# Top-32 attention and a cosine-gated feed-forward on one core: another way of searching the scores, and split, gates and second product at other places of the slot

## The chip, the cores and the metric

The kernel runs on one core of one Trainium2 chip. The metric is the device time of one execution in microseconds (us): the median of three runs.

## The reference

Scores are formed for 8 batches of 8 heads with 576 queries and 576 keys of 64 numbers. In each row all but the 32 largest scores are masked out; the row goes through a softmax and is multiplied with v. The result, 4608 tokens of 512 numbers, goes through two products with a gate between them.

```python
def _attn_ref(q, k, v):
    scores = scale * np.matmul(q, k.transpose(0, 1, 3, 2))
    kth = np.partition(scores, -top_k, axis=-1)[..., -top_k:-top_k + 1]
    scores = np.where(scores >= kth, scores, -1000000000.0)
    scores = scores - np.max(scores, axis=-1, keepdims=True)
    attn = np.exp(scores)
    attn = attn / (np.sum(attn, axis=-1, keepdims=True) + 1e-09)
    return np.matmul(attn, v)

def _moe_ref(x, w_in, w_out):          # 4608 x 512, 512 x 2048, 2048 x 512
    h = x @ w_in
    g = h * np.cos(h)
    return g @ w_out
```

## The kernel before, in words

**Units, slots and blocks.** A unit is 128 queries of a pair of heads: 144 units. A block is the 128 tokens of four units (36 blocks); the feed-forward works by blocks. The program is a list of 144 slots, one for each unit, written out by hand in `slot` (the schedule is manual: each engine gets its instructions in the order of the code, and an instruction that waits holds up all that stand behind it on its engine). In slot i the unit u = i is searched, the unit w = i - 1 is masked and exponentiated, the unit x = i - 2 is split, and parts of the feed-forward of earlier blocks are laid between, by the remainder m of i by four. Slots of remainder 0 to 3 are called s0 to s3 below.

**Scores.** TensorE forms the scores of two units in each even slot (`scores`, L242); a score buffer of a unit is free again when VectorE has folded it. ScalarE copies them into SBUF (`take_scores`, L253 and L257) at the end of the slot before the search.

**The search.** A row of 576 scores is folded at its middle: the larger of each pair by VectorE straight from the score buffer (`fold_high`, L267), the smaller by GpSimd as sum minus larger, in whole numbers (`fold_sum` L283, `fold_low` L292), or by VectorE in the three slots of `BUSY`, in which weights are still being decoded (`fold_now`, L275). The instruction MAX8 gives the eight largest of a row, MATCH_REPLACE8 strikes them out (`search`, L361 and L366). The 288 larger ones are searched four times for eight, 32 in all, and the 288 smaller ones twice, 16 in all; two reductions over pairs of the two sorted lists (`merge_first` L349, `merge_second` L354) give the 32nd of all, the threshold. GpSimd's smaller half is wanted late, when the larger half has been searched through.

**Mask, exponentials, split.** ScalarE masks (L380) and exponentiates (L389, with the sum of the row), loading its table anew when a sine stood between. VectorE forms sum and reciprocal (L397, L402) in the last search of the slot. `send` then runs at the start of the next slot but one after the search: GpSimd splits the weights into 16-bit halves (L412) and copies the reciprocal beside them (L418), SP writes the halves out (L446), issues loads of later q, k and v, and reads the halves back transposed into a ring of five places (L452). The first units go through TensorE instead (`turn`).

**P@V and the feed-forward.** In s2 TensorE multiplies the four units of a block with v (`values`, L480), and VectorE scales them into xT (L496, L504). The first product of a block has four banks of 64 matmuls (`first_bank`, L543); ScalarE takes each bank twice, as h / 2 pi and rounded to a whole number (`take_first`, L557 and L559); GpSimd forms the argument (`argument`, L572 and L575), ScalarE the sine of two banks at a time (`sine`, L583), GpSimd the gate, which overwrites the bank (`gate`, L592). The second product has four runs of 16 matmuls, one for each gated bank (`second_run`, L606), and is taken out and stored by ScalarE (`take_second`, L616 and L618). Banks and second product share two PSUM buffers. The order of the feed-forward of one block over the slots before the change:

| slot | first product | second product | GpSimd |
|---|---|---|---|
| s2 | bank 0 | | |
| s3 | bank 1 | | |
| s0 | bank 2 | | arguments 0, 1 |
| s1 | bank 3 | run 0 | gates 0, 1, argument 2 |
| s2 | | run 1, behind P@V of the next block | argument 3, gates 2, 3 |
| s3 | | run 2 | |
| s0 | | run 3, then taken out | |

Of the kernel before, what the change touches and what calls it, by code (L numbers as in the profile page):

```python
# [10 lines left out]
F32 = mybir.dt.float32  # L11
I32 = mybir.dt.int32
# [3 lines left out]
ALU = mybir.AluOpType  # L16
# [14 lines left out]
def kernel(  # L31
# [218 lines left out]
    def take_scores(u):  # L250
# [7 lines left out]
        if at:  # L258
            nc.scalar.copy(out=s[:, :, 0:at], in_=u["sc"][:, :, 0:at])  # L259

    def fold_high(u):

        s, sc = u["s"], u["sc"]
        if u["n"] not in BUSY:
            del u["sc"]
        u["rest"] = work.tile([P, 2, S], F32, tag="rest", name="rest", bufs=1)
        nc.vector.tensor_tensor(  # L267
            out=u["rest"][:, :, HS:S], in0=sc[:, :, 0:HS], in1=s[:, :, HS:S], op=ALU.max
        )

    def fold_now(u):

        s, sc = u["s"], u.pop("sc")
        u["low"] = work.tile([P, 2, HS], F32, tag="low", name="low", bufs=1)
        nc.vector.tensor_tensor(  # L275
            out=u["low"], in0=sc[:, :, 0:HS], in1=s[:, :, HS:S], op=ALU.min
        )

    def fold_sum(u):

        s = u["s"].bitcast(I32)
        u["low"] = work.tile([P, 2, HS], F32, tag="low", name="low", bufs=1)
        nc.gpsimd.tensor_tensor(  # L283
            out=u["low"].bitcast(I32), in0=s[:, :, 0:HS], in1=s[:, :, HS:S], op=ALU.add
        )

    def fold_low(u):

        if u["n"] in BUSY:
            return  # L290
        low = u["low"].bitcast(I32)
        nc.gpsimd.tensor_tensor(  # L292
            out=low, in0=low, in1=u["rest"][:, :, HS:S].bitcast(I32), op=ALU.subtract
        )

    dens = []
    for i in range(2):
# [3 lines left out]

    tops = []
    for i in range(2):
        t = consts.tile([P, 2, TOPK + 1, 2], F32, tag=f"top{i}", name=f"top{i}")
        nc.vector.memset(t[:, :, 0, 1], -NEG)
        tops.append(t)

    def topk_first(u, w, ahead=()):  # L310

        u["top"] = tops[u["n"] % len(tops)]
        if w:
            merge_first(w)
        for step in ahead:
            step()
        if u["n"] not in BUSY:
            fold_sum(u)
        fold_high(u)
        if w:  # L320
            merge_second(w)
        if u["n"] in BUSY:
            fold_now(u)
        topk_round(u, 0, [lambda: distances(w), lambda: None] if w else ())

    def topk_round(u, rnd, between=(), ahead=None):
        top, rest, lasts = u["top"], u["rest"], TOPK // 8 - 1
        end = TOPK - 1 - 8 * rnd
        at = top[:, :, end : end - 8 if rnd < lasts else None : -1, 0]
        search(  # L330
            at, rest[:, :, HS:S] if rnd == 0 else rest[:, :, 0:HS], rest[:, :, 0:HS], rnd < lasts,
            between if rnd < lasts else (),
        )
        if rnd < lasts:
            return
        del u["rest"]
        low = u.pop("low")
        for k in range(TOPK // 16):
            more = k < TOPK // 16 - 1
            if ahead and not more:  # L340
                ahead()
            search(top[:, :, 1 + 8 * k : 9 + 8 * k, 1], low, low, more, () if more else between)

    def merge_first(u):
        n = TOPK // 2 + 1
        u["lesser"] = u["top"].rearrange("p j r i -> p j (r i)")[:, :, 2 * n : 3 * n]
        nc.vector.tensor_reduce(  # L349
            out=u["lesser"], in_=u["top"][:, :, 0:n], axis=mybir.AxisListType.X, op=ALU.min  # L350
        )

    def merge_second(u):
        nc.vector.tensor_reduce(  # L354
            out=u["top"][:, :, TOPK - 1, 1], in_=u.pop("lesser"), axis=mybir.AxisListType.X,
            op=ALU.max, negate=True,
        )

# [7 lines left out]
                nc.vector.match_replace(rest[:, j], to[:, j], src[:, j], NEG)  # L366

    def distances(u):
        top = u.pop("top").rearrange("p j r i -> p j (r i)")
        u["less"] = top[:, :, 2 * TOPK - 1 : 2 * TOPK]  # L370
        u["nd"] = small.tile([P, 2], F32, tag="nd", name="nd")
        nc.vector.tensor_reduce(
            out=u["nd"], in_=top[:, :, 2 * TOPK - 2 : 2 * TOPK], axis=mybir.AxisListType.X, op=ALU.add
        )

    def mask(u):
# [27 lines left out]
    def both(u):  # L404
        return [lambda: sums(u), lambda: reciprocal(u)] if u else ()

    def split_scores(u):
# [4 lines left out]
        nc.gpsimd.tensor_copy(out=halves[:, :, 0 : 2 * S], in_=s.rearrange("p (k h) -> p h k", h=2))  # L412

    def split_sums(u):

        halves = u["halves"]
        rden = u.pop("rden").bitcast(U16).rearrange("p (j h) -> p h j", h=2)
        nc.gpsimd.tensor_copy(  # L418
            out=halves[:, :, 2 * S :].rearrange("p h (j d) -> p h j d", j=2),
            in_=rden.unsqueeze(3).to_broadcast([P, 2, 2, D]),  # L420
        )
# [216 lines left out]
    at_slot, at_once = {}, {}  # L638

    def load_at(i, *what):  # L640
        while i in at_slot or (what[0] is load_v and i % NP == 0):
            i += 1
        at_slot[i] = what

# [17 lines left out]
    for i, u in enumerate(units):  # L662
        u["n"] = i

    def send(x, between=()):

        split_scores(x)
        split_sums(x)
        for step in between:
            step()  # L670
        write_halves(x)
        for load, b, hp in at_send.pop(x["n"] + 2, ()):
            load(b, hp)
        transposes(x)

    def slot(i, u, w, x, z):
        m, b = i % NP, (i - NP - 2) // NP
        n = (3, 4, 3, 4, 4, 3, 2, 2, 0, 2, 2, 0)[i] if i < 3 * NP else 0
# [12 lines left out]
        topk_round(u, 1)  # L691
        topk_round(u, 2)
        if i > 1:
            decode_second(NP)
            decode_third()

        for o in scored.get(i, []):
# [54 lines left out]
        decode_first(NP)  # L752

    def drain():

        b = NB - 2
        ff["end"] = True
        w, x, last_two = units[NU - 1], units[NU - 2], units[NU - 2 :]
        send(x)
        argument(b, 0)  # L760
        second_run(b - 1, 3)
        merge_first(w)
        merge_second(w)
        distances(w)
        mask(w)
        exponentials(w)
        sums(w)
# [1 line left out]
        send(w)  # L769
        take_first(b, 1)  # L770
        argument(b, 1)
        first_bank(b, 2)
        sine(b, 0)
        gate(b, 0)
        gate(b, 1)
        take_second(b - 1)
        take_first(b, 2)
        first_bank(b, 3)
        argument(b, 2)
        second_run(b, 0)  # L780
        take_first(b, 3)
# [2 lines left out]
        sine(b, 1)  # L784
        gate(b, 2)
        gate(b, 3)
        values(units[NU - 4 : NU - 2])
        take_values(units[NU - 4 : NU - 2])
        second_run(b, 2)
        values(last_two)  # L790
        take_values(last_two)
        second_run(b, 3)
        b += 1
        first_bank(b, 0)
        take_second(b - 1)
        take_first(b, 0)
        argument(b, 0)
        for k in range(1, BANKS):
            first_bank(b, k)
            take_first(b, k)  # L800
            argument(b, k)
            if k % 2 == 1:
                sine(b, k // 2)
                gate(b, k - 1)
                gate(b, k)
# [55 lines left out]
```

## Time and profile before

| | |
|---|---|
| median of three runs | 1406.32 us (1405.22 to 1406.49) |
| the profiled execution | 1406.25 us |
| its span on the core | 1404.1 us |
| granted TensorE clock, mean | 0.985 |
| ScalarE busy | 1140.7 us (81%) |
| GpSimd busy | 1197.8 us (85%) |

The busy time of TensorE is modelled from pipelined matmuls; whether it stands still is read from the starts of its groups. A row of the timeline gives start and length in us, engine, line, operation, tiles, shape and count, and in brackets the idle time before it with what ended it. A row of the stretches gives the stretch, its length, and the busy time of TensorE, its weight loads, VectorE, ScalarE and GpSimd with their numbers of instructions, then granted clock, DMA share and GB/s. A grouped row gives line, engine, operation, tiles and shape with its count, then busy time and mean ns of one, then idle time before. PE is TensorE, DVE VectorE, ACT ScalarE, POOL GpSimd, SP SyncE.

### The profile page before, as it was taken

The page shows a single profiled execution, that of the slowest core. Times are in us where ns is not written, and L with a number is a line of the kernel's source. Part 1 is how long each engine was busy: PE and PEld are TensorE (multiplying, and loading weights), DVE is VectorE, ACT ScalarE, POOL GpSimd, SP SyncE. Part 2 cuts the span into 40 slices and gives each one's busy share as a digit, 9 for nine tenths or more (in the row PEclk, how much of TensorE's full clock was granted, in tenths as well). Part 3 has the DMA queues.
Part 4 walks back from the last instruction along what each step waited for, and adds up shares of the span by engine and source line. Part 5 has one row for each costly group of instructions (what it writes and reads, how often), then busy time and mean ns, then how long its engine had stood idle before and what let it go on. Part 6 is the DMA issues. An engine that isn't in the chain of part 4 may idle for free.

```text
span 1404.1 us, 43874 instructions
## 1 busy us (share of the span) xinstructions
PE 1347.3 (96%) x17024; PEld 906.3 (65%) x17024; DVE 1337.5 (95%) x5012; ACT 1140.7 (81%) x2043; POOL 1197.8 (85%) x1008
## 2 busy tenths in 40 slices
PE   5569999999999999999999999999999999999998
PEld 3355666666666666666666666666666666776665
DVE  7998999999999999999999999999999999999941
ACT  6978888888888888888888888888888888888842
POOL 4787999999999999999999999999999999999920
PEclk9789999999999999999999999999999999999999
DMA  9567775768566586767756568666768566555640
GB/s 285 191 195 188 191 191 152 200 177 200 165 167 168 158 195 172 182 166 176 193 165 176 151 171 198 165 176 163 207 169 175 145 165 172 156 155 144 159 121 16
DMA packets 427488, 240.87 MB, mean 172 GB/s; under 512 B 375952, under 2 KB 392592, under 8 KB 427280
## 3 DMA queue, kind: packets, MB, share of 16 engines
q1 hardware_dynamic: 420720, 224.22, 61.2%
q10 hardware_dynamic: 6560, 13.85, 3.0%
q8 instruction: 133, 2.18, 0.7%
q14 instruction: 75, 0.61, 0.1%
HBM read 45.09 MB, written 101.19 MB: 104 GB/s over the span
## 4 chain that ended last, share of the span: by engine, by line
DVE 68%; ACT 18%; PE 8%; POOL 3%; issue 1%; DMA 1%; ACTq 0%; POOLq 0%; DVEq 0%
DVE top L361 32%; DVE rest L366 18%; DVE rest L267 7%; DVE low L366 6%; ACT s L389 4%; ACT s L380 4%; PE o L606 3%; ACT L583 3%; PE mm L543 3%; ACT x L583 2%; ACT s L253 2%; PE rim L480 2%; ACT s L257 2%; DVE xT L496 1%; DMA ring<-rows 1%
## 5 line engine op out<-in xcount | busy, mean ns | idle before, releaser
L543 PEld LDWEIGHTS mm<-xT,w_in 128*64 128x64 f32 x9216 | 509.5, 137 | 68.2 <-issue 30.3
L543 PE MATMUL mm<-xT,w_in 128*64 128x128 f32 x9216 | 523.7, 273 | 2.7 <-ACT x L559 1.7
L606 PE MATMUL o<-w_out,g 128*64 128x512 f32 x2304 | 521.8, 595 | 3.1 <-POOL g L592 3.1
L361 DVE MAX8 top<-rest 128x8 f32<-128x288 f32 x1152 | 478.9, 451 | 0.0
L366 DVE MATCH_REPLACE8 rest<-top,rest 128x288 f32<-128x288 f32 x864 | 376.6, 443 | 0.0
L380 ACT ACTIVATE s<-s,top 128x576 f32<-128x576 f32 x288 | 207.7, 769 | 189.0 <-DVE top L354 130.3
L606 PEld LDWEIGHTS o<-w_out,g 128*64 128x64 f32 x2304 | 160.6, 137 | 257.6 <-issue 253.2
L412 POOL COPY halves<-s 128x2304 uint16<-128x2304 uint16 x140 | 294.6, 2104 | 35.7 <-ACT s L389 22.3
L361 DVE MAX8 top<-low 128x8 f32<-128x288 f32 x576 | 241.8, 449 | 1.5 <-POOL low L292 1.5
L389 ACT ACTIVATE s<-s,nd 128x576 f32<-128x576 f32 x288 | 220.8, 769 | 2.2
L292 POOL TENSOR_TENSOR low<-low,rest 128x576 int32<-128x576 int32 x141 | 199.8, 1417 | 11.0
L283 POOL TENSOR_TENSOR low<-s 128x576 int32<-128x576 int32 x141 | 200.0, 1418 | 6.5 <-ACT s L259 6.5
L592 POOL TENSOR_TENSOR g<-g,x 128x512 f32<-128x512 f32 x136 | 172.5, 1279 | 16.4 <-ACT x L583 16.4
L575 POOL TENSOR_TENSOR x<-g,x 128x512 f32<-128x512 f32 x136 | 174.0, 1279 | 11.4
L242 PE MATMUL sc<-k,q 64*64 64x448 f32 (+1 forms) x1120 | 147.9, 568 | 14.4 <-DMA k<-in_k_dram 7.4
L480 PE MATMUL rim<-ring,v 128*64 128x128 f32 (+1 forms) x2560 | 138.8, 267 | 0.2 <-issue 0.2
L480 PEld LDWEIGHTS rim<-ring,v 128*64 128x64 f32 x2560 | 129.5, 139 | 6.8 <-issue 6.3
L253 ACT COPY s<-sc 128x896 f32<-128x896 f32 (+1 forms) x144 | 128.0, 889 | 3.4 <-PE sc L242 3.4
L366 DVE MATCH_REPLACE8 low<-top,low 128x288 f32<-128x288 f32 x288 | 125.4, 443 | 0.0
L267 DVE TENSOR_TENSOR rest<-sc,s 128x576 f32<-128x576 f32 x144 | 107.7, 748 | 6.8 <-ACT s L259 6.8
L257 ACT COPY s<-rim 64x256 f32<-64x256 f32 (+1 forms) x280 | 102.8, 367 | 6.9 <-PE rim L480 5.2
L242 PEld LDWEIGHTS rim<-k,q 64*64 64x64 f32 (+1 forms) x1120 | 49.0, 139 | 75.6 <-issue 60.1
(55 smaller groups left out, 1210.1 us busy)
## 6 DMA issues: line engine op xcount, KB each, us to landing
rows<-halves SPq DMA_DIRECT2D x140, 640.0 KB, 3.5
out_dram<-ob ACTq DMA_DIRECT2D x36, 256.0 KB, 3.9
q<-in_q_dram SPq DMA_DIRECT2D x31, 288.0 KB, 5.0
st<-in_moe_w_in_dram SPq DMA_DIRECT2D x16, 512.0 KB, 6.9
v<-in_v_dram SPq DMA_DIRECT2D x32, 256.0 KB, 4.4
k<-in_k_dram SPq DMA_DIRECT2D x31, 144.0 KB, 4.5
k<-in_k_dram SPq DMA_DIRECT2D x32, 128.0 KB, 4.4
st<-in_moe_w_out_dram SPq DMA_DIRECT2D x8, 512.0 KB, 5.6
```

What stands on the lines that cost most here:

```text
L242: nc.tensor.matmul(to[r0 : r0 + rows, rim_bank(r0, j) if k0 else place(u["hp"], j), 0 : k1 - k0], st["q"][d, q0 : q0 + rows], st["k"][d, k ...
L267: nc.vector.tensor_tensor(out=u["rest"][:, :, HS:S], in0=sc[:, :, 0:HS], in1=s[:, :, HS:S], op=ALU.max)
L283: nc.gpsimd.tensor_tensor(out=u["low"].bitcast(I32), in0=s[:, :, 0:HS], in1=s[:, :, HS:S], op=ALU.add)
L292: nc.gpsimd.tensor_tensor(out=low, in0=low, in1=u["rest"][:, :, HS:S].bitcast(I32), op=ALU.subtract)
L361: nc.vector.max(to[:, j], src[:, j])
L366: nc.vector.match_replace(rest[:, j], to[:, j], src[:, j], NEG)
L380: nc.scalar.activation(out=s[:, j], in_=s[:, j], func=AF.Prelu, bias=less[:, j], scale=1.0, alpha=FAR)
L389: nc.scalar.activation(out=s[:, j], in_=s[:, j], func=AF.Exp, bias=nd[:, j : j + 1], scale=SCALE, accum_out=den[:, j, 0:1],)
L412: nc.gpsimd.tensor_copy(out=halves[:, :, 0 : 2 * S], in_=s.rearrange("p (k h) -> p h k", h=2))
L480: nc.tensor.matmul(to[d, r], lhsT, rhs, start=(bank, j) not in begun, stop=c == NT - 1 and u in us[-2:] and r0 + rows == P,)
L543: nc.tensor.matmul(mm[r0 : r0 + D, a * P : (a + 1) * P], w_in[f // FC][:, c, (f % FC) * P + r0 : (f % FC) * P + r0 + D], blk["xT"][:, c], ...
L606: nc.tensor.matmul(blk["o"][r0 : r0 + D], g[:, at : at + D], w_out[f], start=f == 0, stop=f == NF - 1)
```

## The change

The larger half is searched twice for eight, with the rest of it written beside the smaller half; what is left of both, 576 numbers in one tile `rest`, is then searched twice for eight more. The 32nd found is the threshold, and one reduction, which changes its sign, takes the place of the two merges. The smaller half is wanted from the third search on. The smaller half is folded by VectorE in every s1 too (`by_vector`).

`send` is called for w instead of x, at the end of the slot of its exponentials. In the feed-forward, runs 0 and 1 of the second product both stand in s1, run 2 in s2 behind P@V, run 3 in s3, and the second product is taken out at the start of ScalarE's work in s0. In s2 the call of run 2 stands ahead of the sine and the gate of its bank, so the run multiplies that bank (a quarter of the 2048 columns) without the cosine, and the gate comes after. In s3, bank 0 is taken out ahead of the mask; in s0, `sine` and the taking of bank 2 stand behind the copy of the scores. The drain after the last slot follows the same order.

```diff
+    def by_vector(u):
+        return u["n"] in BUSY or u["n"] % NP == 1 and u["n"] > NP + 2
...
-    def topk_first(u, w, ahead=()):
+    def topk_first(u, w):
         u["top"] = tops[u["n"] % len(tops)]
+        u["rest"] = work.tile([P, 2, S], F32, tag="rest", name="rest", bufs=1)
         if w:
-            merge_first(w)
-        for step in ahead:
-            step()
-        if u["n"] not in BUSY:
+            threshold(w)
+        if not by_vector(u):
             fold_sum(u)
         fold_high(u)
-        if w:
-            merge_second(w)
-        if u["n"] in BUSY:
+        if by_vector(u):
             fold_now(u)
-        topk_round(u, 0, [lambda: distances(w), lambda: None] if w else ())
+        search(
+            u["top"][:, :, 1:9], u["high"], u["rest"][:, :, 0:HS], True,
+            [lambda: distances(w), lambda: None] if w else (),
+        )

     def topk_round(u, rnd, between=(), ahead=None):
...
+        if ahead:
+            ahead()
+        some = u["rest"][:, :, 0 : HS if rnd == 1 else S]
+        search(u["top"][:, :, 1 + 8 * rnd : 9 + 8 * rnd], some, some, rnd < TOPK // 8 - 1, between)
...
+    def threshold(u):
+        u["less"] = u["top"][:, :, 0:1]
         nc.vector.tensor_reduce(
-            out=u["lesser"], in_=u["top"][:, :, 0:n], axis=mybir.AxisListType.X, op=ALU.min
-        )
...
+            out=u["top"][:, :, 0], in_=u["top"][:, :, TOPK : TOPK + 1], axis=mybir.AxisListType.X,
             op=ALU.max, negate=True,
         )
...
     def slot(i, u, w, x, z):
...
-        if x:
-            (turn if i < NP + 2 else send)(x)
-        if m == 1:
-            gate(b, 0)
-        elif m == 0:
-            argument(b, 0)
-        topk_first(u, w, [lambda: argument(b - 1, 3)] if m == 2 else ())
+        if x and i < NP + 2:
+            turn(x)
+        topk_first(u, w)
         fold_low(u)
...
         if z:
             values(z)
-        if m == 1:
+        if m == 0:
+            take_second(b - 1)
+            first_bank(b, 2)
+        elif m == 1:
+            gate(b, 0)
             gate(b, 1)
-        elif m == 0:
+            argument(b, 2)
+            first_bank(b, 3)
+            second_run(b, 0)
+            second_run(b, 1)
+        elif m == 2:
+            second_run(b - 1, 2)
+        else:
             second_run(b - 1, 3)
-        elif m == 2:
-            second_run(b - 1, 1)
-        elif m == 3:
-            second_run(b - 1, 2)
+            take_first(b, 0)
+            first_bank(b, 1)

         if w:
             mask(w)
+        if m == 2:
+            sine(b - 1, 1)
+            gate(b - 1, 2)
+            gate(b - 1, 3)
+        if w:
+            exponentials(w)
         if m == 0:
             take_first(b, 1)
             argument(b, 1)
-            first_bank(b, 2)
         elif m == 1:
-            take_first(b, 2)
-            argument(b, 2)
-            first_bank(b, 3)
-            second_run(b, 0)
-        if w:
-            exponentials(w)
-        if m == 3:
-            take_first(b, 0)
-        elif m == 2:
-            sine(b - 1, 1)
-            gate(b - 1, 2)
-            gate(b - 1, 3)
+            take_first(b, 3)
         if i + 1 < NU:
             take_scores(units[i + 1])
+        if m == 0:
+            sine(b, 0)
+            take_first(b, 2)
...
         topk_round(u, 3, both(w), ahead)
...
-        if m == 2:
+        if w and i > NP:
+            send(w)
+        if m == 1:
+            argument(b, 3)
+        elif m == 2:
             first_bank(b, 0)
         elif m == 3:
-            first_bank(b, 1)
-        elif m == 0:
-            sine(b, 0)
-            take_second(b - 1)
-        elif m == 1:
-            take_first(b, 3)
+            argument(b, 0)
         decode_first(NP)
```

More of the change, by code (lines that the diff above doesn't have):

```diff
@@ L259, in take_scores @@
             nc.scalar.copy(out=s[:, :, 0:at], in_=u["sc"][:, :, 0:at])
+    def by_vector(u):
+        return u["n"] in BUSY or u["n"] % NP == 1 and u["n"] > NP + 2
     def fold_high(u):
         s, sc = u["s"], u["sc"]
-        if u["n"] not in BUSY:
+        if not by_vector(u):
             del u["sc"]
-        u["rest"] = work.tile([P, 2, S], F32, tag="rest", name="rest", bufs=1)
+        u["high"] = work.tile([P, 2, HS], F32, tag="high", name="high", bufs=1)
         nc.vector.tensor_tensor(
-            out=u["rest"][:, :, HS:S], in0=sc[:, :, 0:HS], in1=s[:, :, HS:S], op=ALU.max
+            out=u["high"], in0=sc[:, :, 0:HS], in1=s[:, :, HS:S], op=ALU.max
         )
@@ L273, in fold_now @@
         s, sc = u["s"], u.pop("sc")
-        u["low"] = work.tile([P, 2, HS], F32, tag="low", name="low", bufs=1)
         nc.vector.tensor_tensor(
-            out=u["low"], in0=sc[:, :, 0:HS], in1=s[:, :, HS:S], op=ALU.min
+            out=u["rest"][:, :, HS:S], in0=sc[:, :, 0:HS], in1=s[:, :, HS:S], op=ALU.min
         )
@@ L281, in fold_sum @@
         s = u["s"].bitcast(I32)
-        u["low"] = work.tile([P, 2, HS], F32, tag="low", name="low", bufs=1)
         nc.gpsimd.tensor_tensor(
-            out=u["low"].bitcast(I32), in0=s[:, :, 0:HS], in1=s[:, :, HS:S], op=ALU.add
+            out=u["rest"].bitcast(I32)[:, :, HS:S], in0=s[:, :, 0:HS], in1=s[:, :, HS:S], op=ALU.add
         )
     def fold_low(u):
-        if u["n"] in BUSY:
+        if by_vector(u):
             return
-        low = u["low"].bitcast(I32)
-        nc.gpsimd.tensor_tensor(
-            out=low, in0=low, in1=u["rest"][:, :, HS:S].bitcast(I32), op=ALU.subtract
-        )
+        low = u["rest"].bitcast(I32)[:, :, HS:S]
+        nc.gpsimd.tensor_tensor(out=low, in0=low, in1=u["high"].bitcast(I32), op=ALU.subtract)
     dens = []
@@ L328, in topk_round @@
[L328 to L342, printed above, removed]
@@ L368, in distances @@
     def distances(u):
-        top = u.pop("top").rearrange("p j r i -> p j (r i)")
-        u["less"] = top[:, :, 2 * TOPK - 1 : 2 * TOPK]
         u["nd"] = small.tile([P, 2], F32, tag="nd", name="nd")
         nc.vector.tensor_reduce(
-            out=u["nd"], in_=top[:, :, 2 * TOPK - 2 : 2 * TOPK], axis=mybir.AxisListType.X, op=ALU.add
+            out=u["nd"], in_=u.pop("top")[:, :, 0:2], axis=mybir.AxisListType.X, op=ALU.add
         )
@@ L405, in both, with split @@
         return [lambda: sums(u), lambda: reciprocal(u)] if u else ()
-    def split_scores(u):
+    def split(u):
         s = u.pop("s").rearrange("p j k -> p (j k)").bitcast(U16)
@@ L640, in load_at @@
     def load_at(i, *what):
-        while i in at_slot or (what[0] is load_v and i % NP == 0):
+        while i in at_slot or (what[0] is load_v and i % NP == 3):
             i += 1
@@ L663, with send @@
         u["n"] = i
[L665 to L670, printed above, removed]
+    def send(x):
+        split(x)
         write_halves(x)
-        for load, b, hp in at_send.pop(x["n"] + 2, ()):
+        for load, b, hp in at_send.pop(x["n"] + 1, ()):
             load(b, hp)
@@ L757, in drain @@
         ff["end"] = True
[L758 to L763, printed above, removed]
+        w, last = units[NU - 1], units[NU - NP :]
+        threshold(w)
         distances(w)
+        take_second(b - 1)
+        first_bank(b, 2)
         mask(w)
@@ L786, in drain @@
         gate(b, 3)
-        values(units[NU - 4 : NU - 2])
-        take_values(units[NU - 4 : NU - 2])
+        values(last)
+        take_values(last)
         second_run(b, 2)
-        values(last_two)
-        take_values(last_two)
-        second_run(b, 3)
         b += 1
         first_bank(b, 0)
-        take_second(b - 1)
         take_first(b, 0)
         argument(b, 0)
+        second_run(b - 1, 3)
+        first_bank(b, 1)
+        take_second(b - 1)
         for k in range(1, BANKS):
-            first_bank(b, k)
             take_first(b, k)
             argument(b, k)
+            if k < BANKS - 1:
+                first_bank(b, k + 1)
             if k % 2 == 1:
```

30 lines of the change are left out of this document (9 added, 21 removed).

## The prediction

> Slots are named by the remainder of their number by four: s0, s1, s2, s3; four slots make a block. All sums are made against the profiled execution, 1406.25 us with a span of 1404.1 us; the median of the three runs is 1406.32.
>
> **What bounds the kernel now.** First the busy shares of the page, then PE's rows of one block in order of time (start, length, line), then VectorE's.
>
> ```profile
> PE 1347.3 (96%) x17024; PEld 906.3 (65%) x17024; DVE 1337.5 (95%) x5012; ACT 1140.7 (81%) x2043; POOL 1197.8 (85%) x1008
> ```
>
> ```profile
> 701.01 0.98 PE L242 MATMUL sc<-k,q 64*64 64x448 f32 x8
> ...
> 702.18 0.98 PE L242 MATMUL sc<-k,q 64*64 64x448 f32 x8
> ...
> 703.20 0.90 PE L480 MATMUL rim<-ring,v_tail 64*64 64x128 f32 x16
> ...
> 707.57 3.60 PE L606 MATMUL o<-w_out,g 128*64 128x512 f32 x16
> 711.00 3.66 PE L543 MATMUL mm<-xT,w_in 128*64 128x128 f32 x64
> 714.50 3.60 PE L606 MATMUL o<-w_out,g 128*64 128x512 f32 x16
> 717.93 3.66 PE L543 MATMUL mm<-xT,w_in 128*64 128x128 f32 x64
> 721.52 0.98 PE L242 MATMUL sc<-k,q 64*64 64x448 f32 x8
> ...
> 723.62 3.65 PE L606 MATMUL o<-w_out,g 128*64 128x512 f32 x16
> ...
> 737.63 0.98 PE L242 MATMUL sc<-k,q 64*64 64x448 f32 x8
> ```
>
> The same place of the order comes back after 737.63 - 701.01 = 36.62 us. Start to start, a run of the second product takes 3.43 (707.57 to 711.00), a bank of the first 3.50, P@V 4.37 (703.20 to 707.57), a block's four scores 2.19 + 2.10. With four runs and four banks that is 36.4: PE stands still for 0.2 us in a block.
>
> ```profile
> 701.38 0.75 DVE L267 TENSOR_TENSOR rest<-sc,s 128x576 f32<-128x576 f32 x1
> ...
> 711.16 0.75 DVE L267 TENSOR_TENSOR rest<-sc,s 128x576 f32<-128x576 f32 x1
> ...
> 712.74 0.07 DVE L366 MATCH_VALUE_LOAD rest<-top,rest 128x8 f32 x1
> ...
> 713.16 0.08 DVE L366 MATCH_VALUE_LOAD rest<-top,rest 128x8 f32 x1
> ...
> 713.59 0.81 DVE L361 MAX8 top<-rest 128x8 f32<-128x288 f32 x2
> ...
> 714.32 0.07 DVE L366 MATCH_VALUE_LOAD rest<-top,rest 128x8 f32 x1
> ...
> 720.08 0.75 DVE L267 TENSOR_TENSOR rest<-sc,s 128x576 f32<-128x576 f32 x1
> ```
>
> The folds of two units stand 8.92 us apart, and 9.78 where the slot also forms xT (s2): 36.6 a block, without a gap. PE and VectorE are both full; neither alone can give more than the other lets through.
>
> **The change part by part.**
>
> *The search.* A MAX8 of 288 takes 0.365 from start to start (713.59 to 714.32 for two), a replacement with its load 0.42 (712.74 to 713.16).
>
> ```profile
> L361 DVE MAX8 top<-rest 128x8 f32<-128x288 f32 x1152 | 478.9, 451 | 0.0
> L361 DVE MAX8 top<-low 128x8 f32<-128x288 f32 x576 | 241.8, 449 | 1.5 <-POOL low L292 1.5
> ...
> L496 DVE TENSOR_TENSOR xT<-rim,ring 128x256 f32<-128x256 f32 x30 | 12.0, 419 | 11.4 <-PE rim L480 10.0
> ...
> L496 DVE TENSOR_TENSOR xT<-rim,ring 128x512 f32<-128x512 f32 x14 | 9.7, 692 | 2.0 <-ACT s L257 0.7
> ```
>
> Per unit that is 12 MAX8 and 8 replacements now; then 8 (four of 288, four of 576) and 6 (four and two). No search of 576 stands in the trace; the nearest rows are the products of 256 and 512, 273 ns apart, so 288 elements more cost 0.30. A MAX8 of 576 is then 0.665 and a replacement 0.72, and a unit saves 4 x 0.065 + 2 x 0.12 = 0.50 us. If 576 costs twice 288, it saves nothing: that is the other end. One of the two merges goes, 0.14 (143.00 to 143.14 below). The slot falls to 8.93 - 0.64 = 8.29. A second fold on VectorE in each s1 gives 0.66 back (143.14 to 143.80), and takes 2.9 us from POOL.
>
> ```profile
> 143.00 0.23 DVE L349 TENSOR_REDUCE top<-top 128x34 f32<-128x68 f32 x1
> 143.14 0.75 DVE L267 TENSOR_TENSOR rest<-sc,s 128x576 f32<-128x576 f32 x1
> 143.80 0.18 DVE L354 TENSOR_REDUCE top<-top 128x2 f32<-128x34 f32 x1
> ```
>
> By work alone a block would need 34.7 us of VectorE, and PE with 36.4 would bound.
>
> *The new waits.* Three changes of order decide. (1) The smaller half is now wanted before round 2, 4.0 us into the slot, instead of 6.4; POOL's two folds may begin only when the unit before has left `rest`. (2) The split moves behind the last round of the slot before, so its small copy, which waits for the reciprocal, and an `argument` behind it stand ahead of the next fold on POOL. (3) In s2, second_run(b-1, 2) is now recorded ahead of gate(b-1, 2): PE reads that bank ungated, and the gate on POOL, which overwrites it, must wait for the run's last matmul. Behind it in POOL's order stand gate 3, the split, the small copy and both folds of s3. POOL's rows:
>
> ```profile
> 700.25 2.10 POOL L412 COPY halves<-s 128x2304 uint16<-128x2304 uint16 x1
> ...
> 708.05 2.52 POOL L592 TENSOR_TENSOR g<-g,x 128x512 f32<-128x512 f32 x2 [0.54 <-ACT x L583]
> ...
> 712.56 0.39 POOL L418 COPY halves<-rden 128x256 uint16<-128x256 uint16 x1
> 712.92 1.40 POOL L283 TENSOR_TENSOR low<-s 128x576 int32<-128x576 int32 x1
> 714.41 1.42 POOL L292 TENSOR_TENSOR low<-low,rest 128x576 int32<-128x576 int32 x1
> ...
> 720.03 0.40 POOL L418 COPY halves<-rden 128x256 uint16<-128x256 uint16 x1 [1.29 <-DVE rden L402]
> 720.40 0.62 POOL L572 TENSOR_SCALAR x<-x 128x512 f32<-128x512 int32 x1
> ...
> 722.34 1.41 POOL L283 TENSOR_TENSOR low<-s 128x576 int32<-128x576 int32 x1
> ```
>
> The row at 720.03 shows what a waiting instruction does there: POOL stands 1.29 us, and everything behind it with it.
>
> On SP the rows and the transposes of a unit go out at the end of a slot instead of early in the next:
>
> ```profile
> rows<-halves SPq DMA_DIRECT2D x140, 640.0 KB, 3.5
> ```
>
> P@V in s2 wants the rows that leave at the end of s0, a whole s1 (8.95) and 2 us more before it: hidden, for nothing; without that cover it would cost what is missing of landing and transpose, up to 1.5.
>
> Now the chain, from the start of s2:
> - threshold 0.12; the fold frees the score buffer, and PE's second scores start 0.80 after the fold began (701.38 to 702.18): 0.92.
> - Scores 1.02, P@V 4.37, the run 3.60 to its end, 0.05 to POOL: 9.96.
> - Two gates 2.52, split 2.10, small copy 0.36, first fold 1.49 (712.92 to 714.41), second 1.42: 17.85.
> - VectorE's round 2 (2 x 0.665 + 2 x 0.72 = 2.77) and round 3 with sums and reciprocal (1.51): s0 starts at 22.15. s2 itself ends at 10.4, so s3 takes 11.8 in place of 8.9.
> - s0: small copy 0.46 after its start, argument 1.94 (720.40 to 722.34), folds 2.91, then 4.28 of VectorE: 9.6.
> - s1, all on VectorE: 8.29 + 0.66 = 8.95.
>
> The block takes **40.7 us**, 4.1 more than now. The way through s1's first gate (copy 0.46, gate 1.25, about 0.3 to PE, two runs 6.86, scores 1.05: 9.9 against 8.95 + 0.92) is as long, so I take 40.8. ScalarE, at 81%, has its mask of s3 put behind PE's bank 0, but ends the exponentials some 2.5 us before round 3 asks for them. All of (1) to (3) priced at nothing gives 36.4; a search of 576 at twice 288, 0.5 more in each slot, gives 42.7.
>
> *The clock.* PE would stand 4.4 us in a block: some 2.5 before run 0 in s1, 1.9 between the scores in s0. Stretches of 3.4 us, with PE's busy time behind their length and the granted clock third from the end:
>
> ```profile
> 68.40:71.80 3.40, 1.91 (x26) 1.19 (x28) 3.40 (x15) 3.40 (x7) 3.40 (x3) 1.00 0.90 316
> 71.80:75.20 3.40, 3.40 (x68) 3.40 (x66) 3.40 (x14) 3.37 (x9) 3.32 (x4) 1.00 0.61 179
> 102.50:105.90 3.40, 1.26 (x6) 0.57 (x8) 3.40 (x14) 3.35 (x7) 3.40 (x5) 1.00 1.02 407
> 105.90:109.30 3.40, 3.40 (x10) 1.20 (x8) 3.40 (x14) 3.36 (x8) 3.30 (x3) 0.50 0.27 84
> ```
>
> With 1.5 us idle the next stretch kept its clock; with 2.1 idle it fell to half for a stretch, which costs 1.7 us of PE's work. A gap of 2.5 leaves that much idle in one stretch in about half of its positions. One block in two at 1.7, on the path through s1: 0.85, between 0 and 1.7. [...]
>
> *Start and drain.* Up to 143.14 thirteen units have been searched, with VectorE as the limit (third busy time, 39.34 of 40):
>
> ```profile
> 40.00:80.00 40.00, 25.39 (x274) 19.11 (x274) 39.34 (x141) 35.38 (x72) 30.96 (x24) 0.74 0.56 184
> ```
>
> That is -0.64 each, and a few waits for folds behind weight decoding: -4 in all, between -9 and +6. The drain holds one run less for PE, but the last search ends later in the block: 0, between -6 and +6.
>
> **The sum.** From the fold of unit 13 to that of unit 143 are 130 slots:
>
> ```profile
> 1332.99 0.75 DVE L267 TENSOR_TENSOR rest<-sc,s 128x576 f32<-128x576 f32 x1
> ```
>
> 1332.99 - 143.14 = 1189.9 now. Then 32 blocks x (40.8 + 0.85) + s1 and s2 (8.95 + 10.4) = 1352.2, so +162.3; with -4 and 0: 1406.25 + 158.3 = **1564.5 us**.
>
> **The rivals.**
> 1. *Faster.* The folds on POOL keep ahead of VectorE and PE's 36.4 bounds: 0.2 x 32.5 = 6.5 less, start 8 less: 1392. It decides from the point at which s3's second fold ends within 4 us of its slot, that is, if gate 2 is free by 5 us into s2. For it: POOL loses 2.9 us a block. Against it: the run cannot end before 9.9.
> 2. *Gate 2 does not hold POOL, the early demand for the folds still does.* s2 and s0 stay at 10.4 and 9.6, s3 falls to about 9.7: 38.65 a block, 32 x 38.65 + 19.35 - 1189.9 = +66: 1468. Against it: nothing but the run's end releases that write.
> 3. *As forecast, but the clock holds*: 40.8: 1537.
> 4. *The clock falls in each block, or the 576 searches are dear*: 42.5: 1592.
>
> **How the numbers follow.** Forecast 0.45, rival 3 0.2, rival 4 0.2, rival 2 0.09, rival 1 0.06. The range 1500 to 1605 takes in 3 and 4 with the bounds of start and drain and leaves out 1 and 2. A difference of 0.2% is about what a measurement of this kernel can tell from none. Faster 0.06, the same 0.01, slower 0.93.
>
> **What would show it.** POOL idle before the gate in s2, released by PE's second product, some 4 us in 34 blocks; VectorE idle before a MAX8 of round 2, released by POOL's second fold, longest in s3 (some 3 us), about 1.4 in s2 and s0 and none in s1; folds 8.9, 10.4, 11.8, 9.6 apart; half clocks spread over the span. PE at 99% in the middle, or VectorE never waiting for POOL, would make it wrong.

## The result, and the profile after

The changed kernel takes **1593.45 us** (median of four runs, 1590.2 to 1597.62) where the kernel before took 1406.4: 1.133 times as long, with an interval of 1.130 to 1.136. The profiled execution took 1590.2 us with a span of 1588.4.

Busy shares, the granted clock in 40 slices, the chain that ended last by engine, and two groups of the page:

```profile
PE 1392.4 (88%) x17024; PEld 921.6 (58%) x17024; DVE 1284.7 (81%) x3746; ACT 1144.3 (72%) x2043; POOL 1113.5 (70%) x944
...
PEclk6789899999999989999999989999999998999999
...
DVE 36%; POOL 23%; PE 17%; ACT 15%; DMA 3%; issue 3%; SPq 1%; POOLq 0%; ACTq 0%
...
L339 DVE MAX8 top<-rest 128x8 f32<-128x576 f32 (+1 forms) x864 | 533.7, 650 | 181.8 <-POOL rest L294 181.8
L579 PE MATMUL o<-w_out,g 128*64 128x512 f32 x2304 | 528.0, 607 | 67.8 <-POOL g L565 63.9
```

No engine is full any more. VectorE is busy for 53 us less than before, since the search saves more than the folds that it took over cost, and stands 182 us before the MAX8 of round 2, waiting for POOL's second fold. The kernel has gone from two full engines to a chain that passes from one engine to the next. The waits, with the sum, their number and the longest:

```profile
POOL g L565 <- PE o L579: 192.9, 33, 12.9
DVE top L339 <- POOL rest L294: 181.8, 101, 4.3
...
POOL halves L391 <- DVE rden L378: 118.7, 95, 2.1
...
PE sc L242 <- DMA k<-in_k_dram: 30.0, 9, 5.2
PEld sc L242 <- DMA q<-in_q_dram: 25.5, 6, 6.0
```

One block in order of time shows the first two. POOL, then the folds and the waiting MAX8 of VectorE, then PE:

```profile
672.59 1.42 POOL L294 TENSOR_TENSOR rest<-rest,high 128x576 int32<-128x576 int32 x1
678.46 2.51 POOL L565 TENSOR_TENSOR g<-g,x 128x512 f32<-128x512 f32 x2 [4.45 <-PE o L579]
680.91 2.11 POOL L388 COPY halves<-s 128x2304 uint16<-128x2304 uint16 x1
682.95 0.40 POOL L391 COPY halves<-rden 128x256 uint16<-128x256 uint16 x1
683.31 1.42 POOL L285 TENSOR_TENSOR rest<-s 128x576 int32<-128x576 int32 x1
684.81 1.42 POOL L294 TENSOR_TENSOR rest<-rest,high 128x576 int32<-128x576 int32 x1
```

```profile
659.86 0.76 DVE L271 TENSOR_TENSOR high<-sc,s 128x576 f32<-128x576 f32 x1
...
668.77 0.76 DVE L271 TENSOR_TENSOR high<-sc,s 128x576 f32<-128x576 f32 x1
...
674.04 1.42 DVE L339 MAX8 top<-rest 128x8 f32<-128x576 f32 x2 [1.18 <-POOL rest L294]
675.38 0.07 DVE L344 MATCH_VALUE_LOAD rest<-top,rest 128x8 f32 x1
...
676.10 0.08 DVE L344 MATCH_VALUE_LOAD rest<-top,rest 128x8 f32 x1
...
679.62 0.75 DVE L271 TENSOR_TENSOR high<-sc,s 128x576 f32<-128x576 f32 x1
...
686.26 1.42 DVE L339 MAX8 top<-rest 128x8 f32<-128x576 f32 x2 [2.56 <-POOL rest L294]
...
690.62 0.75 DVE L271 TENSOR_TENSOR high<-sc,s 128x576 f32<-128x576 f32 x1
...
700.27 0.76 DVE L271 TENSOR_TENSOR high<-sc,s 128x576 f32<-128x576 f32 x1
```

```profile
674.70 3.60 PE L579 MATMUL o<-w_out,g 128*64 128x512 f32 x16
678.17 3.71 PE L516 MATMUL mm<-xT,w_in 128*64 128x128 f32 x64
...
701.98 4.51 PE L579 MATMUL o<-w_out,g 128*64 128x512 f32 x20 [2.21 <-POOL g L565]
```

POOL has folded for s2 by 674.0 and could gate bank 2, whose sine ScalarE ended at 672.9; it stands 4.45 us until run 2 (674.70) has read that bank, and then has two gates, a split and a small copy to do before it folds for s3. VectorE waits 2.56 us there. The folds stand 8.91, 10.85, 11.00 and 9.65 us apart (s1, s2, s3, s0): 40.41 for this block, and 17 of the 32 blocks behind unit 13 take 40.40 to 40.44.

Of the others three single blocks take 1.65 more, and at four places, some 380 us apart, three blocks in a row take 13 to 17 more together. One such place, SP's queue and PE's scores:

```profile
554.55 0.34 SPq L419 DMA_DIRECT2D rows<-halves  x1
554.94 0.43 SPq L199 DMA_DIRECT2D q<-in_q_dram  x1
555.42 1.11 SPq L203 DMA_DIRECT2D k<-in_k_dram  x1
```

```profile
560.07 2.83 PE L242 MATMUL sc<-k,q 64*64 64x448 f32 x3 [4.19 <-DMA k<-in_k_dram]
```

The loads of q and k go out 0.4 us behind the rows of a unit, and the rows wait on SP for POOL's small copy (547.0 us over the span in 132 waits, the longest 16.2). POOL is late, so the loads are late, and PE stands 4.19 us for them. They also go with another unit: `send` now takes the loads under the key n + 1 in place of n + 2, that is with the rows of the unit after, one slot later than before.

### The profile page after: what moved, and what is told of

Its sections match the earlier page's. It is cut to its first block, busy times and chain, and to the rows that moved or that the text cites. A ratio compares the mean times of both kernels' runs of the same rounds, so it can differ in the third digit from the quotient of the medians.

```text
span 1588.4 us, 42561 instructions
## 1 busy us (share of the span) xinstructions
PE 1392.4 (88%) x17024; PEld 921.6 (58%) x17024; DVE 1284.7 (81%) x3746; ACT 1144.3 (72%) x2043; POOL 1113.5 (70%) x944
## 4 chain that ended last, share of the span: by engine, by line
DVE 36%; POOL 23%; PE 17%; ACT 15%; DMA 3%; issue 3%; SPq 1%; POOLq 0%; ACTq 0%
DVE top L339 20%; DVE rest L344 10%; PE o L579 7%; POOL rest L294 6%; POOL rest L285 5%; POOL halves L388 5%; PE rim L453 4%; PE mm L516 3%; ACT s L365 3%; ACT s L356 3%; POOL x L548 2%; DVE high L271 2%; ACT L365 2%; PE sc L242 2%; DMA k<-in_k_dram 2%
## 5 line engine op out<-in xcount | busy, mean ns | idle before, releaser
L339 DVE MAX8 top<-rest 128x8 f32<-128x576 f32 (+1 forms) x864 | 533.7, 650 | 181.8 <-POOL rest L294 181.8
L516 PE MATMUL mm<-xT,w_in 128*64 128x128 f32 x9216 | 533.4, 276 | 2.7 <-ACT x L532 1.8
L344 DVE MATCH_REPLACE8 rest<-top,rest 128x288 f32<-128x288 f32 (+1 forms) x576 | 337.1, 593 | 0.0
L242 PE MATMUL sc<-k,q 64*64 64x448 f32 (+1 forms) x1120 | 167.3, 577 | 93.0 <-DVE high L271 52.4
L530 ACT ACTIVATE g<-mm 128x512 f32<-128x512 f32 x144 | 84.4, 586 | 207.6 <-PE mm L516 206.0
L294 POOL TENSOR_TENSOR rest<-rest,high 128x576 int32<-128x576 int32 x108 | 154.0, 1426 | 8.5
L285 POOL TENSOR_TENSOR rest<-s 128x576 int32<-128x576 int32 x108 | 152.9, 1416 | 9.0 <-ACT s L259 5.6
L391 POOL COPY halves<-rden 128x256 uint16<-128x256 uint16 x140 | 56.3, 402 | 118.8 <-DVE rden L378 118.7
L339 DVE MAX8 top<-high 128x8 f32<-128x288 f32 x288 | 127.1, 455 | 3.7
L242 PEld LDWEIGHTS sc<-k,q 64*64 64x64 f32 (+1 forms) x1120 | 39.5, 137 | 149.7 <-DVE high L271 58.5
```

The lines of the kernel that those rows point to most:

```text
L242: nc.tensor.matmul(to[r0 : r0 + rows, rim_bank(r0, j) if k0 else place(u["hp"], j), 0 : k1 - k0], st["q"][d, q0 : q0 + rows], st["k"][d, k ...
L285: nc.gpsimd.tensor_tensor(out=u["rest"].bitcast(I32)[:, :, HS:S], in0=s[:, :, 0:HS], in1=s[:, :, HS:S], op=ALU.add)
L294: nc.gpsimd.tensor_tensor(out=low, in0=low, in1=u["high"].bitcast(I32), op=ALU.subtract)
L339: nc.vector.max(to[:, j], src[:, j])
L516: nc.tensor.matmul(mm[r0 : r0 + D, a * P : (a + 1) * P], w_in[f // FC][:, c, (f % FC) * P + r0 : (f % FC) * P + r0 + D], blk["xT"][:, c], ...
```

## The experiments

H in the expectations is the theory of the prediction, that gate 2 on POOL waits for run 2 and holds all behind it; L, that loads queue behind rows on SP.

**Run 2 behind the gates of s2**, where the gated bank is read.

```diff
-        elif m == 2:
-            second_run(b - 1, 2)
...
             gate(b - 1, 2)
             gate(b - 1, 3)
+            second_run(b - 1, 2)
```

> The changed kernel with run 2 of the second product recorded behind gates 2 and 3 in s2, so that the run waits for the gate and the gate no longer for the run (the cosine of that bank is then applied, as in the kernel before). Theory H (the gate that waits for the run holds GpSimd, and with it the folds of s3): VectorE's wait for the fold falls from about 2.8 us to near 0 in s3, a block from 40.4 to about 39.0 us, 32 blocks: some 45 us less, about 1548. Rival D (the folds wanted before round 2 and the split at the end of the slot cost it all, and the gate's wait only fills time in which GpSimd had nothing to do): within 10 us of 1593.

Measured: 1513.46 us, ratio 1.076 (1.074 to 1.078), 80 less than the changed kernel. A regular block takes 38.62 us, 1.8 less: s3 falls from 11.02 to 8.53, and s0 grows from 9.65 to 10.27. The gain is larger than expected: of the 80 us the regular blocks give 58 (1.8 in each of 32, where 1.4 was expected), the three single blocks that had taken 1.65 more give 5, the four long places, which stay, get 13 shorter, and start and drain give the rest. The clock now falls nowhere but at the long places.

**Gate 2 left out** (the second product reads bank 2 without its cosine).

```diff
             sine(b - 1, 1)
-            gate(b - 1, 2)
             gate(b - 1, 3)
```

> The changed kernel without gate 2 (the multiplication of bank 2 by its cosine, which the second product there never reads). Nothing on GpSimd then waits for run 2; 1.25 us of GpSimd's work a block goes too. H: gate 3 runs in s2 by some 15 us of the block, s3 loses its wait for the fold, 38.4 to 38.7 us a block: about 1530 to 1540. D: 1585 to 1593, since the folds of s2 and s0 wait as before.

Measured: 1499.3 us, ratio 1.066 (1.065 to 1.068); a block takes 38.05. That is 31 us below the range of H, as the first experiment was below its own, but far from D: the hold goes whether the gate is left out or run 2 is put behind it.

**The loads ahead of the rows**, first at the start of the same slot, then a slot earlier ahead of the split (the diff of the second).

```diff
     def send(x):
+        for load, b, hp in at_send.pop(x["n"] + 2, ()):
+            load(b, hp)
         split(x)
         write_halves(x)
-        for load, b, hp in at_send.pop(x["n"] + 1, ()):
-            load(b, hp)
         transposes(x)
```

> The changed kernel with the loads of q, k and v issued at the start of the same slot, ahead of the rows that wait for GpSimd's small copy, as in the kernel before. Theory L (four stretches of two to three blocks, each 13 to 15 us longer than the regular 40.4 a block, are score matmuls that wait for q and k behind those rows): the four stretches go, 40 to 55 us less, 1540 to 1553, the regular block stays at 40.4. Rival (the stretches come from the clock, which falls in each of them): 1580 to 1593, the stretches stay.

> The changed kernel with each load of q, k and v issued at the end of the slot before, ahead of the split and so ahead of the rows that wait for it: about one slot earlier than in the changed kernel. L (the stretches are loads that come late because SP waits with the rows in front of them; the start of the slot gave back about half, since SP was still at the transposes of the unit before): the stretches go, the regular 40.4 stays, 1535 to 1550. Rival (loads and transposes disturb each other on the DMA queues wherever they are put): the stretches stay at 6 us or more each, 1560 or above.

Measured: 1561.82 us (ratio 1.112, 1.109 to 1.115) and 1546.9 (1.100, 1.098 to 1.102). At the start of the same slot they still stand behind the transposes of the unit before, and blocks of 44 to 46 us remain; a slot earlier none is left over 42.7, and of the waits of scores for q and k one row remains:

```profile
PE sc L242 <- DMA k<-in_k_dram: 6.1, 2, 5.4
```

The first lies between its two expectations, the second within that of L. So the loads cost 46.6 us, and the way is SP's queue, one unit's rows and transposes too late. A regular block stays at 40.44.

**Both repairs.** Run 2 behind its gate, and the loads a slot earlier: the first diff and the last one together.

> The changed kernel with both repairs: run 2 behind its gate, and the loads a slot earlier. If hold and late loads are separate terms, their savings add: 38.6 a block without stretches, about 1470 to 1485. If the late loads only showed because the block was held, the second repair gives less than 15 us on top of the first (1513).

Measured: 1471.11 us, ratio 1.046 (1.044 to 1.048): 75.8 less than with the loads alone, where run 2 alone gave 80.0, so the two hardly overlap. All 32 blocks take 38.6 us, and the clock falls in none of them.

**The kernel before with the order of the runs alone**: runs 0 and 1 in s1, run 2 in s2 ahead of its gate (bank 2 is read without its cosine), run 3 in s3, and the second product taken out at the start of s0 (not in the diff shown); search and split as before.

```diff
             second_run(b, 0)
+            second_run(b, 1)
...
         elif m == 2:
-            second_run(b - 1, 1)
-        elif m == 3:
             second_run(b - 1, 2)
+        elif m == 3:
+            second_run(b - 1, 3)
```

> The kernel before with one part of the change: runs 0 and 1 in s1, run 2 in s2 ahead of its gate (it reads that bank without the cosine), run 3 in s3, the second product taken out at the start of s0. Old search, old place of the split. H: s3 waits about 3 us for its folds (wanted 6.4 us into the slot), 39.5 to 40.0 us a block in place of 36.6: 1500 to 1515. D: the old search leaves the folds time enough, within 10 us of 1406.

Measured: 1573.02 us, ratio 1.117 (1.114 to 1.120). The wait that it adds, and three stretches of 3.41 us around one gap (length, busy time of PE and of its weight loads, VectorE, ScalarE, POOL, then the granted clock):

```profile
POOL g L592 <- PE o L606: 234.0, 34, 8.4
```

```profile
600.57:603.99 3.42, 3.42 (x64) 3.21 (x60) 3.42 (x14) 3.22 (x5) 3.34 (x3) 1.00 0.40 76
603.99:607.40 3.41, 0.04 (x2) 0.00 (x0) 3.41 (x14) 2.68 (x5) 3.33 (x5) 1.00 1.01 308
607.40:610.81 3.41, 3.28 (x8) 1.12 (x10) 3.41 (x13) 3.38 (x7) 3.33 (x4) 0.50 0.44 86
```

The order of the runs alone takes a block from 36.6 to 39.95 (four blocks). PE stands 3.3 to 3.5 us in one piece in 28 of the 32 blocks, and in 27 of these the clock falls for one or two stretches, which makes them 41.3 to 42.9. The 32 blocks take 56 us more than 32 of 39.95 would. The expectation had left the clock out, hence its miss.

**The kernel before with the new search alone**, and with the second fold of s1 on VectorE as in the change.

> The kernel before with the new search alone (and the smaller half of each s1 folded by VectorE); split, gates and second product where they were. H's chain with the split and the argument still ahead of the folds: s2 waits for the fold until about 11.3 us after its start, s0 9.7, s1 8.9, s3 8.3: 38.0 to 38.3 a block, 1445 to 1462. Rival R (the new search saves VectorE 0.6 us a unit and costs nothing by itself; only the new order does): 36.4 a block, 1390 to 1400.

Measured: 1426.64 us, ratio 1.015 (1.014 to 1.017): between the two expectations. The slots s0 to s3 take 9.64, 8.91, 10.30 and 8.36. In s3, where nothing waits, the search saves 0.57 of 8.93. In s0 and s2 it loses 0.7 and 0.5, by one wait, which POOL's order explains:

```profile
DVE top L341 <- POOL rest L294: 81.2, 68, 2.7
```

```profile
691.06 0.40 POOL L396 COPY halves<-rden 128x256 uint16<-128x256 uint16 x1 [1.56 <-DVE rden L380]
691.43 0.62 POOL L550 TENSOR_SCALAR x<-x 128x512 f32<-128x512 int32 x1
692.13 1.28 POOL L553 TENSOR_TENSOR x<-g,x 128x512 f32<-128x512 f32 x1
693.36 1.42 POOL L285 TENSOR_TENSOR rest<-s 128x576 int32<-128x576 int32 x1
694.86 1.41 POOL L294 TENSOR_TENSOR rest<-rest,high 128x576 int32<-128x576 int32 x1
```

An argument, 1.93 us from 691.43 to 693.36, stands ahead of the folds, as it did before the change, when nobody wanted the folds so soon.

**Folds, then arguments, then the split** in s0, s2 and s3, in that last kernel.

> As the run with the new search alone, but in s2, s3 and s0 GpSimd does the two folds first, then arguments, then the split of the unit two back. H: no fold is late, TensorE's 36.4 a block bounds, about 6 us less in the middle and up to 8 at the start: 1390 to 1402. Rival (the split, later in its slot by 3 us or more, makes its rows late for P@V in s2): 37 or more a block, 1415 or above.

Measured: 1568.79 us, ratio 1.116 (1.114 to 1.118): H fell, the rival stands. The folds no longer hold s0 (8.37), but the split is late: it now stands behind a fold, and POOL stands before that fold until VectorE has formed the reciprocal of the unit before (first row).

```profile
POOL rest L285 <- DVE rden L380: 232.1, 71, 6.1
...
POOL halves L390 <- DMA rows<-halves: 94.0, 27, 5.1
...
PE rim L458 <- DMA ring<-rows: 59.7, 30, 3.8
```

P@V waits 2 us a block for rows, s2 takes 13 to 19 us, and the clock falls in 19 blocks of 32. Both the arguments and the split were moved here; the next run moves the arguments alone.

**Only the arguments behind the folds, and, by itself, the second fold of s0, s1 and s2 on VectorE**, both in the kernel with the new search alone.

```diff
         fold_low(u)
+        if m == 0:
+            argument(b, 0)
+        elif m == 2:
+            argument(b - 1, 3)
```

> The kernel before with the new search and the second fold of s1 on VectorE (as in the run of the search alone, 1426.6 us, slots 9.64, 8.91, 10.30, 8.36), and the arguments of s0 and s2 recorded behind the second fold instead of ahead of the first; the split stays where it is. Theory F (s0 and s2 are long only because an argument of 0.6 to 1.9 us stands between the split's small copy and the folds on POOL): s0 falls to about 8.4 and s2 to about 9.2, VectorE needs 34.9 in a block and PE's 36.4 bounds: 36.4 to 36.6 a block, 1397 to 1406 us. Rival R (the small copy's wait for the reciprocal alone holds the folds): s0 and s2 stay above 9.0 and 9.8, the block above 36.8: 1412 or more. Rival G (the arguments come late for the gates, as rows came late where the split was moved as well): PE waits for POOL's gates and the block is above 37.5: 1435 or more.

> The kernel before with the new search, and the second fold on VectorE in s0, s1 and s2 instead of s1 alone. Theory F (in the run of the search alone s0 and s2 wait for POOL's second fold and for nothing else): s0 8.29 + 0.66 = 8.95, s1 8.95, s2 9.8, s3 8.36, that is 36.1 of VectorE in a block, PE's 36.4 bounds: 36.4 to 36.6 a block, 1397 to 1406 us. Rival R (the wait moves on to the score buffer, to POOL's gates or to rows that come late): 36.9 a block or more, 1415 or more.

Measured: **1389.48 us**, ratio 0.989 (0.987 to 0.990), and 1396.78, 0.993 (0.991 to 0.995): both a little faster than the kernel before, by 1.1% and 0.7%, and just below the range of F. The page of the first, with its busy shares, the chain that ended last by engine, and VectorE's searches:

```profile
PE 1332.7 (96%) x17024; PEld 901.2 (65%) x17024; DVE 1275.1 (92%) x3747; ACT 1142.6 (83%) x2043; POOL 1112.4 (80%) x942
...
PE 89%; DVE 4%; DMA 3%; ACT 2%; POOL 2%; issue 0%; SPq 0%; ACTq 0%; POOLq 0%
...
L341 DVE MAX8 top<-rest 128x8 f32<-128x576 f32 (+1 forms) x864 | 532.9, 649 | 6.0 <-POOL rest L294 4.0
```

The wait for the folds is gone, PE is the bound again (89% of the chain), and a block takes 36.14 us (36.30 with the folds on VectorE). So the search by itself is worth what PE leaves to be won, once POOL folds in time; and what ruined the run before was the split behind the folds, not the arguments.

**The same two cures on the changed kernel with both repairs.**

> The changed kernel with both repairs (run 2 behind the gates, q/k/v loads a slot earlier: 1471 us, 38.62 a block with s0 10.26, s1 8.92, s2 10.90, s3 8.52), and the second fold on VectorE in s0, s1 and s2. Theory F (what is left, 2.0 a block over before, is VectorE's wait for folds that stand behind gates, split and arguments on POOL): the block falls to 36.4 to 37.0, 1395 to 1420 us. Rival P (PE's own order, with the gates and the runs of one slot one behind the other, keeps s0 and s2 long): 37.8 a block or more, 1443 us or more.

> The changed kernel with both repairs (1471 us, 38.62 a block: s0 10.26, s1 8.92, s2 10.90, s3 8.52), and the arguments of s0 and s2 behind the second fold on POOL. Theory F (in s0 and s2 the MAX8 of round 2 waits 1.8 and 1.2 us for a fold that stands behind an argument): s0 falls by 1.8 to about 8.5, s2 by 1.2 to 9.7, a block takes 36.6, bounded by PE, and the time is 1397 to 1412 us. Rival P (the gates of s1, one behind the other, keep PE and with it xT of s2 late, as s2 stayed at 11.3 with the folds on VectorE): s2 stays above 10.8 and the block above 37.2: 1425 to 1445 us.

Measured: 1433.1 us, ratio 1.019 (1.018 to 1.021), and 1476.5, 1.052 (1.050 to 1.054). With the folds on VectorE a block falls by 1.1 to 37.52, between the two expectations. Its s2 stays at 11.34, where the kernel of 1396.78 us, with the same folds on VectorE and the old order, takes 9.96: VectorE waits there 1.6 us a block before xT for ScalarE's copy of the next scores:

```profile
DVE xT L469 <- ACT s L257: 45.8, 28, 1.7
```

In the kernel of 1396.78 us the same wait is 9.2 us in 28 blocks. With the arguments moved, s0 falls to 8.37 as expected, but s2 rises to 13.2, and nothing is won:

```profile
DVE xT L469 <- ACT s L257: 113.2, 28, 4.8
...
ACT x L556 <- POOL x L548: 79.5, 34, 3.5
```

In the changed order the sine of s2 stands ahead of the exponentials on ScalarE; the late argument holds the sine, the sine holds the exponentials and the copy of the next scores behind them, and VectorE stands 4 us a block before xT until that copy is done. In the kernel of 1389 us the sine stands behind the exponentials, and waits for the argument a sixth as long:

```profile
ACT x L561 <- POOL x L553: 12.7, 34, 0.8
```

## Why the prediction was right, and where not

Sign and range held: 1593 lies between 1500 and 1605, and 29 us above the likeliest. The hold, the main term of the forecast, is what the trace and the runs show; that the total came inside the range was in part luck, as the end of this section shows. By the runs the way from 1406.4 goes in steps: the new search with its early demand, 1426.6 (+20); the rest of the new order with run 2 behind its gate and the loads ahead, 1471.1 (+45); run 2 ahead of its gate, 1546.9 (+76); the loads behind the rows, 1593.45 (+47).

- *The search*: a MAX8 of 576 takes 0.67 from start to start (674.04 to 675.38 for two) and its replacement 0.72 (675.38 to 676.10), as estimated from the products; s3 of the search alone came to 8.36, forecast 8.29.
- *The hold*: confirmed in the trace and by three runs. From s2's fold to s0's lie 21.85 us (668.77 to 690.62), forecast 22.15. Its steps come out too: POOL's gate starts 9.69 after s2's fold (forecast 9.96), and its second fold for s3 ends at 17.46 (forecast 17.85); the 0.05 from the run's end to POOL came out as 0.16 (678.30, modelled, to 678.46). In between, s2 was 0.5 longer than forecast and s3 0.8 shorter: the fold's wait of 1.18 and xT stand in s2. A block took 40.42, forecast 40.8. Rival 2's price without the hold, 38.65, is what the first repair gave, 38.62, but only as a sum: s0 and s2 took 10.27 and 10.91 (priced at 9.6 and 10.4), s3 8.53 (priced at 9.7).
- *The early demand* (1): right, and by itself, in the search alone, it turns the gain of 0.57 a slot into a loss of 0.6 a block.
- *The split's new place* (2): wrong. It put the argument ahead of the folds down to the change, but the rows of before at 720.03 to 722.34 have that order already, and by the code of the kernel with the new search the move of the split alone changes the order neither on POOL nor on SP; no run has it by itself. The wait belongs to (1): the argument costs something because the folds behind it are wanted sooner.
- *PE's bound*: 36.4 was read 0.3 too high. P@V was taken as 4.37 from start to start; in the changed kernel it takes 4.09 (670.61 to 674.70), and the kernel of 1389.48 us, bound by PE, runs a block in 36.14.
- *The clock*: a fall costs 1.65 (42.07 against 40.42), forecast 1.7. It was mis-sized in number: with the loads cured, the clock fell in 7 blocks of 32, not 16, and all that the blocks took over the regular length was 14 us, not 27. The gap in s1 is 2.2 us, not 2.5, and behind unit 13 of the changed kernel the falls came behind stretches of 3.41 us with 1.99 to 2.45 idle (the least at 581.68, the most at 936.66 and 1315.54): a gap of 2.2 leaves 1.99 in one stretch only where nearly all of it lies there. Rival 4's number, 1592, is the nearest of all to the result, but neither of its conditions held: the clock did not fall in each block, and a search of 576 was not dear.
- *The step that failed* is SP's: rows and transposes were taken as hidden, for nothing, and the loads of q and k that stand behind them were not priced. They moved from one unit's rows to the next one's, a slot later, onto a queue that now waits for a late POOL: 46.6 us.
- *Start and drain*: forecast -4 and 0. The fold of unit 13 begins where it did, and from that of unit 143 to the end are 70.1 us, 71.1 before:

```profile
143.24 0.76 DVE L271 TENSOR_TENSOR high<-sc,s 128x576 f32<-128x576 f32 x1
...
1518.30 0.75 DVE L271 TENSOR_TENSOR high<-sc,s 128x576 f32<-128x576 f32 x1
```

Between the two are 1375.1 us, forecast 1352.2. The block forecast too long (-12) and the falls that did not come (-13) cover half of the loads (+47). Had block and falls come out as forecast, the loads alone would have put the time near 1611, outside the range: that the range held is luck in this part, since errors of both signs met in it.

What stays open is the +45. It is not POOL's folds alone: with these folds on VectorE in both orders, the new order still takes 37.52 us a block where the old one takes 36.30, and 1433.1 us against 1396.8. The difference lies in s2, before xT, in a wait for ScalarE's copy of the scores, which stands behind the sine in the new order; that the sine's place makes this wait is read from the order of ScalarE's instructions, and no run moves the sine back alone.

## What to carry to other kernels

When a step is moved, write down what stands behind it on each queue, and what those instructions feed, DMA loads for a later stage above all: here the loads cost 47 us and the search they have nothing to do with was sound. A cheaper search that wants its input earlier is only a gain if the engine that makes this input has nothing else ahead of it; moving two arguments of 1.9 us in POOL's order turned +1.5% into -1.1%. And an instruction that overwrites what another engine still reads holds everything that stands behind it on its own engine: POOL stood 4.45 us before its gate, and here this cost 76 to 80 us, until the reader was put behind the writer. Last, a time that lands in the forecast range does not show the forecast right in all its terms: here two terms taken too large hid one that was left out.

## What was not expected of the hardware

The clock fell far more often where PE's gap was longer. A gap of 1.57 us in each block (the changed kernel with both repairs) met a fall in none of 32 blocks, one of 2.2 us (the changed kernel with the loads cured) in 7 of 32, and one of 3.3 to 3.5 us (the kernel before with the new order of the runs) in 27 of the 28 blocks that had it; the mean granted clocks of the three executions are 0.977, 0.972 and 0.938. Stretches of the changed kernel, two around one gap, then two around another:

```profile
697.73:701.14 3.41, 2.04 (x38) 1.79 (x34) 3.41 (x10) 3.13 (x6) 2.98 (x4) 1.00 0.58 131
701.14:704.55 3.41, 2.57 (x12) 0.92 (x14) 3.41 (x14) 3.06 (x7) 3.33 (x4) 1.00 0.47 192
779.65:783.06 3.41, 1.31 (x22) 1.01 (x20) 3.41 (x10) 2.87 (x6) 2.98 (x4) 1.00 0.76 211
783.06:786.47 3.41, 3.41 (x10) 0.98 (x8) 3.41 (x13) 3.38 (x7) 3.06 (x4) 0.50 0.35 127
```

Behind the gap of 2.2 us that is split between two stretches (1.37 and 0.84 idle) the clock stayed at 1.00, also from 704.55 to 707.97; a gap of the same length that falls almost wholly into one stretch (2.10 idle) was followed by 0.50 for the whole of the next. Busy times of PE are modelled, so these shares are not exact. The stretch ahead of this fall, at 779.65, was not wholly idle: it was busy for 1.31 us. The half clock that followed lasted from 783.06 to 786.47, 3.41 us; behind unit 13 of this kernel each lasted 3.41 or 10.24.
